# A fixed rank for each of 3,943 operations in place of a list scheduler, in a cluster-attention and two-MoE kernel

## The chip, the cores and the metric

One core of one Trainium2 chip runs the kernel. The metric is the device time of one execution in microseconds, median of several runs. TensorE (PE) does the matrix products and transposes, VectorE (DVE), ScalarE (ACT) and GpSimd (POOL) the work between them, and all data transfers are issued from SyncE's queue (SP). Each of the five takes its instructions strictly in program order.

## What is computed

Attention over 2 x 8 heads, 768 positions of 64, in which a query sees only the keys of its own cluster, and behind it two dense blocks on the 1536 x 512 result:

```python
q_assign = np.argmax(np.einsum('bhsd,hcd->bhsc', q_n, c_n), axis=-1)
k_assign = np.argmax(np.einsum('bhsd,hcd->bhsc', k_n, c_n), axis=-1)
mask = q_assign[:, :, :, None] == k_assign[:, :, None, :]
scores = np.where(mask, scale * np.matmul(q, k.transpose(0, 1, 3, 2)), -1000000000.0)
attn = softmax(scores); x = attn @ v            # (1536, 512)
a = x @ w1; b = x @ w2; x = ((a * b) @ w3) @ w_out
h = x @ w_in; out = (h * np.clip(h + 3.0, 0.0, 6.0) / 6.0) @ moe2_w_out
```

All inputs are float32. A product is made of three passes, each operand being split into a high and a low part.

## The kernel before

The kernel names 3,943 operations and gives each to a `Plan`: its engine (or several it may run on), an assumed duration, what it needs, which ring buffers it takes and drops, and a due time. `Plan.order` (line 888) is a list scheduler: it walks through assumed time, keeps the operations that are ready and have a buffer, and takes the one with the smallest due time; a table `SHIFT` (line 45) moves nearly every due time by hand. For an operation that may run on several engines it also picks the engine. Operations are then written out in that order, so it fixes the order on each of the five queues. Buffers are rings, and which operation takes a buffer next follows from the order too.

The stages, with the names that the steps below use (first the operation, then the program's name in the profile and its line):

- Start. The SP queue loads q (`lq`), k (`lk`), v and the centroids. Per head h: `T` transposes q and k (ptqk, L1194), `qkh` (ACT) and `qkl` (DVE, L1204) split them, `pa` (L1233) multiplies with the centroids, nine steps `oh0` to `oh8` (mostly DVE, some POOL, L1247 to L1263) make the cluster code, and `Ck` and `Cq` put it beside k and q (copies on DVE and ACT for head 0, DMA later). `Ek`, `Dk`, `Dq` are the DMAs that move k and q rows (L1208). `idle` (L1120) are matmuls without use that keep TensorE busy.
- Attention, six chunks c of 128 queries per head. `S1` and `S` (pst, L1332) make the scores in one of two banks, `mx` (DVE, L1344) the maximum, `ex` (ACT, L1351) the exponential; `S` of a chunk needs `ex` of the chunk before. Nine `pT` (ptr, L1367) transpose the result, `ph` (ACT) and `pl` (DVE, L1010) split it, six `av` (L1390) multiply with v.
- Beside it, to fill TensorE: the product of w3 and w_out (`wt` transposes L1601, `wth`, `wtl`, `w` = psw L1629) and the products with w1 and w2 for half of the tokens (`ab` = psab L1705, which waits for finished heads).
- Each weight block passes a conversion of five steps: load (`ld`, L1550), `c0` and `c2` on ACT, `c1` (a clamp, L1569) on POOL or DVE, `c3` and `c5` on DVE (L1578, L1582). There are 72 of them.
- Then `Wh`, `Wl` (Whl: high and low part of the w3-w_out product), `x2` (psx, L1820), `b` (psab, L1957) for the second half of the tokens, `x2` again, and the second block in 16 groups p: `h` (psh, L2268) in seven products, copies `s` of their banks (m_sn, ACT), `ca`, `hr`, `hm`, `hh`, `hl` (splitting the result into m_gv, m_whl), and `o` (po, L2312). Its weights come back by DMA (`ff`, `wf`) and are split by `Lh`, `Ll`, `woh2`, `wol2`.

TensorE's queue mixes these, so that one stage's waits are covered by another's products.

Of the kernel before, what the change touches and what calls it, by code (L numbers as in the profile page):

```python
# [27 lines left out]
LAT = {  # L28
    ("pe", "act"): 0.2, ("pe", "dve"): 0.2, ("pe", "pe"): 0.0, ("act", "dve"): 0.155, ("act", "pool"): 0.17,
    ("dve", "act"): 0.13, ("act", "pe"): 0.17, ("dve", "pe"): 0.24, ("pool", "pe"): 0.21, ("pool", "pool"): 0.1,  # L30
        ("dve", "dve"): 0.13, ("dve", "pool"): 0.155, ("pool", "act"): 0.08,
}

# [11 lines left out]
SHIFT = {  # L45
    "id": 8.27, "root": -37.83, "warm": -0.72, "cenl": -28.31, "cen1": -21.13, "cen2": -11.74, "cen3": 0.22,
    ("idle", 0): 0.14, ("idle", 1): 14.27, ("idle", 7): -19.93, ("idle", 8): 1.32, ("cT", 0): -2.63,
    ("cTc", 0): -18.72, ("cTc", 1): 38.21, ("lq", 0): -20.58, ("lk", 0): -6.84, ("vhi", 0): 13.43,
    ("vlo", 0): -8.33, ("T", 0, 0): -2.21, ("qkh", 0, 0): -20.39, ("qkl", 0, 0): -48.81, ("T", 0, 1): 58.8,
# [15 lines left out]
    ("vlo", 1): -17.06, ("T", 1, 0): 6.25, ("qkh", 1, 0): -6.73, ("qkl", 1, 0): 36.07, ("T", 1, 1): 0.16,  # L65
# [17 lines left out]
    ("lv", 2): -6.03, ("vhi", 2): -11.41, ("vlo", 2): 0.27, ("T", 2, 0): 24.8, ("qkh", 2, 0): 10.9,  # L83
# [786 lines left out]
class Plan:  # L870
# [1549 lines left out]
```

## Time and profile before

| | us |
|---|---|
| median of 3 runs (761.2 to 762.37) | 761.59 |
| the profiled execution | 763.72 |
| its span, first to last instruction | 761.8 |
| PE busy, of the span | 739.7 |
| DVE busy | 617.8 |
| ACT busy | 551.5 |
| POOL busy | 209.9 |
| mean granted TensorE clock, of full speed | 0.996 |

The span is what the rows below are timed in, from its own zero. A row of a timeline gives start, length, engine, line, operation, output and inputs, count, and in brackets how long the engine sat idle just before and what ended that.

### The profile page before, as it was taken

The numbers are of one execution on the slowest core, as the hardware profiler recorded it, in microseconds if no ns is written. First come the engines' busy times: TensorE is split into PE (matmuls) and PEld (weight loads), VectorE is DVE, ScalarE is ACT, GpSimd is POOL, SyncE is SP. The second block draws the span as 40 slices with busy tenths as digits, with TensorE's granted clock in tenths as the row PEclk, the third lists the DMA queues.
The fourth block names the chain that finished last, engine by engine and source line by source line (L and its number), as shares of the span: only waits on it lengthen the run. The fifth ranks groups of instructions, "written<-read, shape, count | busy, mean of one in ns | idle before, by whom it ended". The sixth has DMA issues, their size and how long they took to land.

```text
span 761.8 us, 12047 instructions
## 1 busy us (share of the span) xinstructions
PE 739.7 (97%) x4143; PEld 673.7 (88%) x4143; DVE 617.8 (81%) x1032; ACT 551.5 (72%) x1037; POOL 209.9 (28%) x232
## 2 busy tenths in 40 slices
PE   5899998999999999999999999999999999999998
PEld 4679887889899998999999999988988888988896
DVE  7778898999988887878896998979878867676642
ACT  6788898888889777878756767668765756565553
POOL 2441645252445435351341301322203000000000
PEclk9999999999999999999999999999999999999999
DMA  8745554565546646342536534685431224222102
GB/s 223 225 128 163 146 146 118 156 160 136 151 124 173 170 127 182 113 137 84 159 100 193 178 125 139 196 264 192 157 103 37 76 70 135 83 60 78 47 1 97
DMA packets 81740, 101.96 MB, mean 134 GB/s; under 512 B 30960, under 2 KB 56592, under 8 KB 81680
## 3 DMA queue, kind: packets, MB, share of 16 engines
q1 hardware_dynamic: 81680, 101.20, 45.0%
q8 instruction: 33, 0.54, 0.3%
q14 instruction: 27, 0.22, 0.1%
HBM read 71.34 MB, written 15.78 MB: 114 GB/s over the span
## 4 chain that ended last, share of the span: by engine, by line
PE 82%; DVE 6%; ACT 5%; DMA 4%; issue 2%; SPq 0%; POOL 0%; DVEq 0%; ACTq 0%; POOLq 0%
PE po L2312 15%; PE psh L2268 13%; PE av L1390 8%; PE psx L1820 8%; PE pst L1332 8%; PE ptr L1367 7%; PE psab L1705 7%; PE psab L1957 7%; PE psw L1629 5%; DMA qkn<-in_k_dram 1%; PE pa L1233 1%; PE ptqk L1194 1%; DVE den L1344 1%; PE pt L1601 1%; DMA rdb<-rd 1%
## 5 line engine op out<-in xcount | busy, mean ns | idle before, releaser
L1569 POOL TENSOR_SCALAR cvt<-cvt 128x512 f32<-128x512 f32 x72 | 67.3, 938 | 192.0 <-ACT cvt L1013 178.1
L1344 DVE TENSOR_REDUCE den<-pst 128x1 f32<-128x768 f32 x96 | 91.5, 953 | 22.8 <-PE pst L1332 18.1
L1351 ACT ACTIVATE p<-pst,den 128x768 f32<-128x768 f32 x96 | 86.6, 902 | 17.8 <-DVE den L1344 16.9
L1010 DVE TENSOR_TENSOR pl<-ptr,ph 128x512 fp32r<-128x512 f32 x135 | 89.4, 680 | 9.4 <-ACT ph L1013 9.1
L1013 ACT ACTIVATE ph<-ptr 128x512 fp32r<-128x512 f32 x135 | 78.7, 596 | 18.6 <-PE ptr L1367 13.8
L1367 PE MATMUL ptr<-id_f,p 128*128 128x128 f32 x576 | 81.3, 272 | 0.9 <-DVE pl L1010 0.6
L1705 PE MATMUL psab<-xT,abhl 128*128 128x384 f32 x384 | 78.9, 342 | 0.3 <-ACT asb L1013 0.3
L1367 PEld LDWEIGHTS ptr<-id_f,p 128*128 128x128 f32 x576 | 68.2, 140 | 8.8 <-DVE pl L1010 0.9
L1332 PE MATMUL pst<-kk,qkL 128*128 128x512 f32 (+1 forms) x192 | 71.0, 378 | 3.1 <-ACT p L1351 3.0
L1705 PEld LDWEIGHTS psab<-xT,abhl 128*128 128x128 f32 x384 | 66.2, 188 | 2.3 <-ACT asb L1013 0.8
L1332 PE MATMUL pst<-kk,qkH 128*128 128x512 f32 (+1 forms) x192 | 64.9, 342 | 0.0
L1390 PE MATMUL av<-pl,vs 128*128 128x384 f32 x180 | 61.3, 341 | 2.3 <-DVE pl L1010 2.3
L1390 PE MATMUL av<-ph,vs 128*128 128x384 f32 x180 | 63.3, 351 | 0.2 <-ACT T L1013 0.2
L1578 DVE SCALAR_TENSOR_TENSOR cvs<-cvt,cvs 128x512 int32<-128x512 int32 x72 | 52.4, 735 | 12.7 <-ACT cvs L1013 6.4
L1013 ACT ACTIVATE cvt<-raw 128x512 f32<-128x512 f32 x72 | 48.2, 672 | 11.5 <-DVE cvs L1582 3.8
L2290 ACT ACTIVATE tt<-m_sn,three 128x384 f32<-128x384 f32 x48 | 29.4, 615 | 37.0 <-DVE m_sn L2278 27.7
L1013 ACT ACTIVATE cvs<-raw 128x512 int32<-128x512 uint8 x72 | 47.9, 673 | 6.7 <-DMA set<-cvs 5.2
L1582 DVE SCALAR_TENSOR_TENSOR cvs<-cvt,cvs 128x512 int32<-128x512 int32 x72 | 51.2, 719 | 0.4
L1629 PE MATMUL psw<-woh,wT 128*128 128x512 f32 x128 | 49.3, 411 | 0.0
L1332 PEld LDWEIGHTS pst<-kk,qkL 128*128 128x128 f32 x192 | 36.9, 192 | 9.8 <-ACT p L1351 8.0
L1013 ACT ACTIVATE m_sn<-psh 128x384 f32<-128x384 f32 x64 | 30.8, 483 | 20.0 <-PE psh L2268 19.9
L2312 PE MATMUL po<-m_whl,m_gv 128*128 128x512 f32 x153 | 40.6, 392 | 0.6 <-DVE m_gv L1010 0.6
(198 smaller groups left out, 1829.6 us busy)
## 6 DMA issues: line engine op xcount, KB each, us to landing
raw<-in_moe_w_dram SPq DMA_DIRECT2D x32, 512.0 KB, 3.6
m_gb<-set SPq DMA_DIRECT2D x64, 256.0 KB, 3.3
raw<-in_moe_w_out_dram SPq DMA_DIRECT2D x24, 512.0 KB, 3.5
raw<-in_moe_w_in_dram SPq DMA_DIRECT2D x16, 512.0 KB, 5.1
set<-cvs SPq DMA_DIRECT2D x32, 256.0 KB, 3.1
kk<-qkH SPq DMA_DIRECT2D x16, 384.0 KB, 4.2
abp<-cvs SPq DMA_DIRECT2D x16, 256.0 KB, 2.3
b_gv<-abp SPq DMA_DIRECT2D x16, 256.0 KB, 4.4
```

The lines of the kernel that those rows point to most:

```text
L1010: nc.vector.tensor_tensor(out=out, in0=a, in1=b, op=ALU.subtract)
L1013: nc.scalar.activation(out=out, in_=in_, func=AF.Copy, **kw)
L1332: x = mm(out=psr[:, t, ks_], lhsT=TT[nm, h][:, i, cs_], rhs=flat(TT["K", h][:, a])[:, ks_], start=st, stop=sp)
L1344: done["mx", n] = [other_banks(nc.vector.tensor_reduce(out=den_at(h, 0, c), in_=psS[h, c], axis=AX.X, op=ALU.max, negate=True), ("S", n + 1))]
L1351: done["ex", n] = [other_banks(nc.scalar.activation(out=flat(p), in_=psS.pop((h, c)), func=AF.Exp, bias=den_at(h, 0, c), accum_out=den_at( ...
L1367: nc.tensor.transpose(pt[:, blk(j)], pps[h, 3 * hf + c][:, blk(kb)], id_f)
L1390: mm(out=t[:, 0:HF], lhsT=vs_t[h][:, 2 * s + i, :], rhs=x_[:, c0:c0 + HF], start=(s == 0 and i == 0 and n == 0), stop=(s == 2 and i == 1 a ...
L1569: (nc.gpsimd.tensor_scalar if e == "pool" else ts)(out=tf, in0=tf, scalar1=H_MAX, scalar2=-H_MAX, op0=ALU.min, op1=ALU.max)
L1629: mm(out=ps, lhsT=wT[m, hf][:, a, blk(kk)], rhs=w_[hf][:, kk, :], start=(kk == 0 and n == 0), stop=(kk == 3 and n == 2))
L1705: mm(out=ps[:, 0:HF], lhsT=s[:, w, a, blk(kk)], rhs=xT0[0][:, x_, kk, hf * HF:hf * HF + HF], start=(kk == 0 and n == 0), stop=(kk == KD - ...
L2268: mm(out=ps[:, 0:HF], lhsT=left(p, l, a, kk), rhs=x[:, x_, kk, :], start=(st and kk == 0 and m == 0), stop=(kk == 1 and m == 2), skip_grou ...
L2312: mm(out=outs[b, c], lhsT=g[:, a, blk(c % 3)], rhs=w[:, w_, :], start=(first and a == 0 and w_ == 0), stop=(last and a == 1))
```

## The change

`SHIFT`, `LAT` and the scheduler go. In their place stand a table `RANK` (for each family of operations one number per operation, its place among all 3,943) and a table `ON` (for each operation that may run on several engines, a letter: a, d, p for ACT, DVE, POOL). `Plan.order` reads both and checks them. Two lists of needs get longer: `gsh` names both operations `abg` that it reads, and `g1sh` all eight `bg1`. The operations are the same; 64 of them stand on another engine. Of the 72 clamps `c1`, 28 go from POOL to DVE. Of `wol2` eight go from DVE to POOL and two back, of `Ll` five and three back, of `Wl` two go to POOL (three of four are there then), and of `woh` two go to DVE. All lines after the tables move up by 592, so L1332 of before is L740 after.

```diff
-SHIFT = {
-    "id": 8.27, "root": -37.83, "warm": -0.72, "cenl": -28.31, "cen1": -21.13, "cen2": -11.74, "cen3": 0.22,
...
+RANK = {
+    "id": "4",
+    "root": "52",
+    "warm": "558",
...
+ON = {
...
+    "c1": "ppdppppppdppddpdpppppppppppdpddppdpppdddpppppddddpdpdpppdppddddppddpddpd",
+    "woh": "apddpppa",
+    "Wl": "pdpp",
...
     def order(self):
-        delta, bias = 0.05, {"dve": 0.3, "pool": -0.3}
...
-            pick = None
-            for e in ENG:
-                if cand[e]:
-                    m = min(cand[e])[0] + delta
-                    c = min((d, st, i, k) for st, d, i, k in cand[e] if st <= m)
...
+            f = k[0] if isinstance(k, tuple) else k
+            pos[k] = int(rank[f][n.setdefault(f, 0)])
...
+                o[2] = {"a": "act", "d": "dve", "p": "pool"}[ON[f][m.setdefault(f, 0)]]
...
+        seq = sorted(ops.values(), key=lambda o: pos[o[0]])
...
+        return seq
...
-            op(("gsh", hf, jp), "act", 0.8, lambda hf=hf, jp=jp: g_hi(hf, jp), ("top", ("abg", 2 * jp + 1, hf)), due=d)
+            op(("gsh", hf, jp), "act", 0.8, lambda hf=hf, jp=jp: g_hi(hf, jp), ("top", ("abg", 2 * jp, hf), ("abg", 2 * jp + 1, hf)), due=d)
...
-    last1 = [("bg1", J1 - 1), ("b", J1 - 1, 6, 1)]
+    last1 = [("bg1", j) for j in range(J1)] + [("b", J1 - 1, 6, 1)]
```

Three places show how the queues move. The first is TensorE at the start, before (ptqk x6 is `T` of head 1, ptqk x3 the first half of `T` of head 2, pt is `wt` of the second block of w3, pa is head 1, pst is `S1` of head 0's first chunk):

```order
L1194 MATMUL ptqk<-id_f,qkn 128x128 x6
L1120 MATMUL idle<-id_r 128x512 x2
L1601 MATMUL pt<-id_f,cvs 128x128 x4
L1194 MATMUL ptqk<-id_f,qkn 128x128 x3
L1233 MATMUL pa<-qkH,cT 128x384
L1233 MATMUL pa<-qkL,cT 128x384
L1233 MATMUL pa<-qkH,cT 128x384
L1233 MATMUL pa<-qkL,cT 128x384
L1332 MATMUL pst<-kk,qkL 128x512
```

and in the change, the same engine and place:

```order
L602 MATMUL ptqk<-id_f,qkn 128x128 x6
L528 MATMUL idle<-id_r 128x512 x4
L641 MATMUL pa<-qkH,cT 128x384
L641 MATMUL pa<-qkL,cT 128x384
L641 MATMUL pa<-qkH,cT 128x384
L641 MATMUL pa<-qkL,cT 128x384
L1009 MATMUL pt<-id_f,cvs 128x128 x4
L740 MATMUL pst<-kk,qkL 128x512
```

The transposes of head 2 no longer stand ahead of the first scores; they come behind `S` of the third chunk. The transposes of w3 stand behind `pa`.

The second is TensorE in head 4, before (ptr is `pT`, twelve matmuls for three of them; the two groups av are the first and the second `av` of head 4):

```order
L1367 MATMUL ptr<-id_f,p 128x128 x12
L1390 MATMUL av<-ph,vs 128x384
L1390 MATMUL av<-pl,vs 128x384
L1390 MATMUL av<-ph,vs 128x384
L1390 MATMUL av<-pl,vs 128x384
L1332 MATMUL pst<-kk,qkL 128x256
L1332 MATMUL pst<-kk,qkH 128x256
L1194 MATMUL ptqk<-id_f,qkn 128x128 x3
L1332 MATMUL pst<-kk,qkL 128x512
L1332 MATMUL pst<-kk,qkH 128x512
L1390 MATMUL av<-ph,vs 128x384
L1390 MATMUL av<-pl,vs 128x384
```

and in the change, from the first of these `av`:

```order
L798 MATMUL av<-ph,vs 128x384
L798 MATMUL av<-pl,vs 128x384
L798 MATMUL av<-ph,vs 128x384
L798 MATMUL av<-pl,vs 128x384
L1037 MATMUL psw<-woh,wT 128x512
L1037 MATMUL psw<-wol,wT 128x512
L1037 MATMUL psw<-woh,wT 128x512
L740 MATMUL pst<-kk,qkL 128x512
L740 MATMUL pst<-kk,qkH 128x512
L602 MATMUL ptqk<-id_f,qkn 128x128 x3
L798 MATMUL av<-ph,vs 128x384
L798 MATMUL av<-pl,vs 128x384
```

One operation `w` (three psw) stands now between the two `av`, and `S` (pst 128x256) stands before the first.

The third is GpSimd at the end of attention, before (abhl is `abl`, cvt is `c1`, Whl is `Wl`, xT is the last head pair's product):

```order
L1007 TENSOR_TENSOR abhl<-cvs,abhl 128x512 x2
L1569 TENSOR_SCALAR cvt<-cvt 128x512
L1007 TENSOR_TENSOR Whl<-W_591,Whl 128x1024
L1569 TENSOR_SCALAR cvt<-cvt 128x512
L1448 TENSOR_TENSOR xT_3003<-T,rdb 128x768
```

and in the change:

```order
L415 TENSOR_TENSOR abhl<-cvs,abhl 128x512
L977 TENSOR_SCALAR cvt<-cvt 128x512
L415 TENSOR_TENSOR Whl<-W_588,Whl 128x1024
L977 TENSOR_SCALAR cvt<-cvt 128x512
L415 TENSOR_TENSOR Whl<-W_588,Whl 128x1024 x2
L856 TENSOR_TENSOR xT_3046<-T,rdb 128x768
```

GpSimd has three `Wl` there in place of one.

## Rows read from the trace of the kernel before

**Rows 1.** The page: busy time, share of the span, instructions of each engine.

```profile
PE 739.7 (97%) x4143; PEld 673.7 (88%) x4143; DVE 617.8 (81%) x1032; ACT 551.5 (72%) x1037; POOL 209.9 (28%) x232
```

**Rows 2.** Busy time by stage: stretch, length, each engine, granted clock, DMA share, GB/s.

```profile
0.00:40.00 40.00, 29.38 (x132) 21.75 (x133) 30.13 (x61) 27.69 (x51) 16.01 (x43) 0.96 0.80 223
110.00:130.00 20.00, 16.93 (x92) 14.20 (x91) 16.65 (x25) 16.21 (x33) 11.31 (x12) 0.91 0.41 117
130.00:190.00 60.00, 59.97 (x376) 53.49 (x376) 57.75 (x98) 50.74 (x102) 19.69 (x24) 1.00 0.59 151
420.00:500.00 80.00, 79.99 (x461) 79.87 (x462) 74.35 (x131) 54.33 (x97) 16.55 (x12) 1.00 0.51 166
500.00:508.00 8.00, 6.63 (x37) 5.99 (x36) 6.23 (x9) 6.52 (x12) 3.10 (x3) 1.00 0.78 250
560.00:645.00 85.00, 83.36 (x416) 74.25 (x415) 66.53 (x110) 53.94 (x96) 8.95 (x5) 1.00 0.23 75
```

**Rows 3.** The same view of four short stretches, two beside each fall of the clock.

```profile
14.80:18.20 3.40, 0.76 (x5) 0.55 (x6) 3.21 (x7) 1.64 (x3) 1.04 (x2) 1.00 1.08 279
18.20:21.60 3.40, 3.40 (x12) 3.17 (x13) 0.93 (x3) 1.75 (x4) 0.60 (x1) 0.51 1.02 304
121.00:124.40 3.40, 1.14 (x5) 0.76 (x4) 3.34 (x5) 2.69 (x6) 1.07 (x2) 0.95 0.00 0
124.40:127.80 3.40, 3.40 (x13) 2.83 (x13) 1.48 (x2) 2.63 (x5) 3.32 (x4) 0.55 0.00 0
```

**Rows 4.** The chain of waits in the first 40 us: start, length, what.

```profile
9.17 1.28 ACT L1092
...
11.81 6.16 DMA qkn<-in_k_dram
```

**Rows 5.** Timelines of the start: PE, then ACT, DVE and POOL.

```profile
18.10 0.76 PE L1194 MATMUL ptqk<-id_f,qkn 128*128 128x128 f32 x3 [2.09 <-DMA qkn<-in_k_dram]
19.94 0.63 PE L1332 MATMUL pst<-kk,qkL 128*128 128x512 f32 x1
10.46 0.20 ACT L1092 ACTIVATE warm<-three 128x1 f32<-128x1 f32 x1
18.25 1.06 ACT L1013 ACTIVATE qkH<-cd 16x384 fp32r<-16x384 f32 x2
10.58 0.58 DVE L1247 STREAM_TRANSPOSE as<-pa 128x384 f32<-128x384 f32 x1 [0.18 <-PE pa L1233]
12.88 0.69 DVE L1578 SCALAR_TENSOR_TENSOR cvs<-cvt,cvs 128x512 int32<-128x512 int32 x1 [0.54 <-ACT cvs L1013]
17.22 0.35 DVE L1054 CAST kk<-cd 16x384 fp32r<-16x384 f32 x1
25.91 1.77 DVE L1578 SCALAR_TENSOR_TENSOR cvs<-cvt,cvs 128x512 int32<-128x512 int32 x1
25.75 1.39 POOL L1007 TENSOR_TENSOR wol<-cvs,woh 128x512 fp32r<-128x512 f32 x1
```

**Rows 6.** Timelines of head 4: PE twice, DVE, POOL.

```profile
118.97 0.66 PE L1367 MATMUL ptr<-id_f,p 128*128 128x128 f32 x4 [0.64 <-DVE pl L1010]
123.80 0.49 PE L1390 MATMUL av<-pl,vs 128*128 128x384 f32 x1 [2.26 <-DVE pl L1010]
119.43 2.85 DVE L1582 SCALAR_TENSOR_TENSOR cvs<-cvt,cvs 128x512 int32<-128x512 int32 x2
119.30 1.83 POOL L1448 TENSOR_TENSOR T<-T,rdb 128x768 f32<-128x768 f32 x1
```

**Rows 7.** Timelines before the second block: PE, then ACT.

```profile
505.67 1.34 PE L2268 MATMUL psh<-m_x1b,m_gB 128*128 128x384 f32 x6 [1.04 <-ACT m_sn L1013]
504.10 1.14 ACT L1013 ACTIVATE m_whl<-m_gb 128x512 fp32r<-128x512 f32 x2
```

**Rows 8.** Groups by line: two on POOL, busy time, mean of one, idle before.

```profile
L1569 POOL TENSOR_SCALAR cvt<-cvt 128x512 f32<-128x512 f32 x72 | 67.3, 938 | 192.0 <-ACT cvt L1013 178.1 <-DVE pl L1010 5.7 <-DVE m_sn L2282 4.3
L1007 POOL TENSOR_TENSOR Whl<-W,Whl 128x1024 fp32r<-128x1024 f32 x1 | 3.2, 3219 | 5.3 <-PE ptr L1367 5.3
```

More of the change, by code (lines that the diff above doesn't have):

```diff
@@ L27 @@
 ENG = ("pe", "act", "dve", "pool", "dma")
[L28 to L32, printed above, removed]
 RUN_ON = {
@@ L867 @@
+ON = {
+    "Ck": "dd",
+    "Cq": "aa",
+    "oh1": "pppdppppppdpdpp",
+    "oh4": "pdppppdppdppppp",
+    "xh": "papa",
+    "c1": "ppdppppppdppddpdpppppppppppdpddppdpppdddpppppddddpdpdpppdppddddppddpddpd",
+    "woh": "apddpppa",
+    "Wl": "pdpp",
+    "gsl": "dddddddp",
+    "bxl": "ddddddd",
+    "bxs": "dddd",
+    "g1s": "dddd",
+    "Ll": "ddddddddddddddddddpdpddddppdpddd",
+    "wol2": "ddpdddddpdddppddddpddpddppdpdddd",
+    "xwl": "dddddddddddddp",
+    "xs": "ddddpddd",
 }
@@ L884, in op @@
             eng, dur = (eng,), (dur,)
-        self.ops[key] = [key, dict(zip(eng, dur)), None, fn, tuple(need), due + SHIFT.get(key, 0.0), tuple(take), tuple(drop), lat,
+        self.ops[key] = [key, dict(zip(eng, dur)), None, fn, tuple(need), due, tuple(take), tuple(drop), lat,
             len(self.ops), lock, tuple(after)]
     def order(self):
-        delta, bias = 0.05, {"dve": 0.3, "pool": -0.3}
-        ops = self.ops
-        left, users, src = {}, {}, {}
+        ops, pos, n, m = self.ops, {}, {}, {}
@@ L892, in order @@
+        rank = {f: v.split() for f, v in RANK.items()}
         for k, o in ops.items():
-            left[k] = len(o[4]) + len(o[11])
-            src[k] = []
-            for n in o[4]:
-                users.setdefault(n, []).append((k, True))
-            for n in o[11]:
-                users.setdefault(n, []).append((k, False))
-        slots = {r: [0.0] * c for r, c in self.rings.items()}
-        free = dict.fromkeys(ENG, 0.0)
-        port = {"dve": 0.0, "pool": 0.0}
-        ready = {k: None for k, o in ops.items() if not left[k]}
@@ L903, in order @@
-        out = []
-        while len(out) < len(ops):
-            cand = {e: [] for e in ENG}
-            for k in ready:
-                o = ops[k]
-                t = 0.0
-                ok = True
-                for r in set(o[6]):
-                    c = o[6].count(r)
-                    if len(slots[r]) < c:
-                        ok = False
-                        break
-                    t = max(t, sorted(slots[r])[c - 1])
-                if not ok:
-                    continue
-                best = None
-                for e, d in o[1].items():
-                    st = max(free[e], t)
-                    for end, pe in src[k]:
-                        st = max(st, end + LAT.get((pe, e), 0.08))
-                    if e == "pool":
-                        st = max(st, port["dve"])
-                    elif e == "dve" and o[10]:
-                        st = max(st, port["pool"])
-                    f = st + d + bias.get(e, 0.0)
-                    if best is None or f < best[0]:
-                        best = (f, e, st)
-                cand[best[1]].append((best[2], o[5], o[9], k))
-            pick = None
-            for e in ENG:
-                if cand[e]:
-                    m = min(cand[e])[0] + delta
-                    c = min((d, st, i, k) for st, d, i, k in cand[e] if st <= m)
-                    if pick is None or c[1] < pick[0]:
-                        pick = (c[1], c[3], e)
-            if pick is None:
-                raise RuntimeError(f"no operation can start after {len(out)} of {len(ops)}")
-            st, k, e = pick
-            o = ops[k]
-            o[2] = e
-            del ready[k]
-            for r in o[6]:
-                slots[r].remove(min(slots[r]))
-            end = st + o[1][e]
-            free[e] = end
-            if e == "pool" or e == "dve" and o[10]:
-                port[e] = end
-            for r in o[7]:
-                slots[r].append(end + 0.3)
-            out.append(k)
-            for u, data in users.get(k, ()):
-                if data:
-                    src[u].append((end + o[8], e))
-                left[u] -= 1
-                if not left[u]:
-                    ready[u] = None
@@ L959, in order @@
-        return [ops[k] for k in out]
+            f = k[0] if isinstance(k, tuple) else k
+            pos[k] = int(rank[f][n.setdefault(f, 0)])
+            n[f] += 1
+            o[2] = next(iter(o[1]))
+            if len(o[1]) > 1:
+                o[2] = {"a": "act", "d": "dve", "p": "pool"}[ON[f][m.setdefault(f, 0)]]
+                m[f] += 1
+            assert o[2] in o[1], k
+        seq = sorted(ops.values(), key=lambda o: pos[o[0]])
+        room = dict(self.rings)
+        for i, o in enumerate(seq):
+            assert pos[o[0]] == i, o[0]
+            assert all(pos[x] < i for x in o[4] + o[11]), o[0]
+            for r in o[6]:
+                room[r] -= 1
+                assert room[r] >= 0, (o[0], r)
+            for r in o[7]:
+                room[r] += 1
```

257 lines of the change are left out of this document (142 added, 115 removed), and 828 rows, old and new, of tables (RANK, SHIFT).

## The prediction

> **What bounds the kernel now.** I read the page's busy times first. TensorE is busy in 739.7 of 761.8 us [rows 1], and the change leaves its operations as they are, so an order can win no more than the 22.1 us in which it idles, and what a slower clock costs it. The view by stage shows where that is: 10.6 us in the first 40, 3.1 in 110 to 130, 1.4 in 500 to 508, 1.6 in 560 to 645 (each length less PE busy [rows 2]). From 130 to 190 and from 420 to 500 it idles for 0.04 us in 140. So most of the kernel is a wall of matmuls that no order shortens, and the case is decided at four short places, and by whether the new order makes new ones.
>
> The same view gives the clock. It stands at 0.51 of full speed, the 1.2 GHz level, from 18.2 to 21.6, after 3.4 us in which TensorE was busy for 0.76, and at 0.55 from 124.4 to 127.8, after 3.4 us with 1.14 busy [rows 3]. Each time some 1.6 us are lost: 3.4 us of matmuls at half speed do the work of 1.7 to 1.9. So an idle time of 2 to 3 us there is paid nearly twice.
>
> Second, VectorE. It is busy for 57.75 of 60 us from 130 to 190 (96%) and 74.35 of 80 from 420 to 500 (93%) [rows 2]. The change gives it more work, so it's the engine to fear.
>
> **The start.** Before, the first scores `S1` begin at 19.94, and just ahead of them TensorE waits 2.09 us for k of head 2, whose load took 6.16 us [rows 4, 5]. The scores need none of it; their own last input is made by the two copies on ACT from 18.25 to 19.31, and the first chunk uses the first, done at about 18.8 [rows 5]. In the new order the transposes of head 2 stand behind the third chunk, and that gate is gone.
>
> What is late next is VectorE. The new order puts `c5` of the first w3 block (0.69, as its neighbour `c3` took [rows 5]) ahead of head 0's split, loads k of head 0 one place later, and puts `c1` and `c3` of the second block ahead of `oh0`. I make that 0.69 for `c5`, 0.69 for `c3`, and for `c1` between 0.35 and 0.69: no clamp ran on VectorE, the nearest rows are its short steps of 0.35 and its conversions of 0.69. Idle time of 0.18 ahead of `oh0` takes some back, and so does the clamp's lying in a wait. `oh0` moves from 10.58 to about 12.0. Behind it `c3` and `wtl` (0.69 each) no longer stand in the chain of codes, so the first copy `Ck` stays at 17.22 + 1.4 - 1.4 = 17.2, the second follows on the same engine (0.35), and `S1` starts at about 18.1: 1.8 us earlier.
>
> From there the chunks of head 0 run as a chain of scores, maximum and exponential, which the earlier start shifts as a whole. Inside it one conversion took 1.77 us in place of 0.69, ending 0.54 after a POOL operation (25.75 + 1.39) that began before it [rows 5]. Whether VectorE meets POOL again there, the order doesn't say; I count 0.4 of the 1.1. Sum: -2.2, bounds 0 (another load gates) and -3.5.
>
> A rule of the Trainium skill speaks against the change here. The load of the exponential's table took 1.28 us at 9.17, beginning 0.02 after the operation before and followed by the next at 10.46 [rows 4, 5]; the new order drops it from there to just ahead of the first exponential. By the same walk it fits: ACT is through with the second `wth` at about 19.1, loads until 20.4, and the maximum comes at about 20.6. The Trainium skill ("ScalarE: Activation LUTs", What ACT_TABLE_LOAD costs) gives a switch of tables 1.28 us and another 1.38 of drain; by that the start would win 1.1 us less. No drain shows in the rows, and the place is the one where it would matter.
>
> **Head 4.** TensorE waits 0.64 us and then 2.26 for `pl` [rows 6], and loses 1.6 to the clock after it. VectorE is late because its two `c5` took 2.85 us, where two of 0.69 are 1.4; POOL's 1.83 us began 0.13 before them. In the new order VectorE has the same sequence (`pl` twice, `c5` twice, `mx`, `pl` twice) and POOL the same two products, so I expect them to meet again. TensorE, however, has one more `w` (three psw) ahead of the second `av` and one more among the transposes. A matmul of all shapes took 0.16 us on average from 130 to 190 (59.97 us in 376 [rows 2]); three are 0.5, and as `w` has the widest shape, 512 columns, I say 0.7; what `S` takes is moved ahead and no longer counts. So the idle 2.9 shrinks by 0.6 and 0.5 to 1.8, and the clock falls or doesn't: half of 1.6. Sum: -1.1 - 0.8 = -1.9, bounds 0 and -4.5 (all of it gone).
>
> **Before the second block.** `h` of the first group waits 1.04 us for the copy of its bank [rows 7], which ACT makes only after a copy of x2 and two weight copies that together take 1.14 [rows 7]. The new order puts this copy ahead of those three. The wait for VectorE's sum behind it stays. Sum: -0.8, bounds 0 and -1.4, the idle time of that stretch.
>
> **The end of attention.** `Wl` on POOL took 3.22 us [rows 8]; the change has three there, so about 9.7 us of POOL inside some 12, beside conversions on VectorE. By the two stretched conversions above, VectorE can't start such an operation while POOL is in one. I price one meeting at the stretch that head 4 shows, 1.4, and count 0.7 of it as reaching TensorE, which has `ab` products to do. Sum: +1.0 for one and a half, bounds 0 (all under `ab`) and +3.2 (one whole `Wl`).
>
> **The rest.** In 560 to 645 TensorE idles 1.6 us, mostly at an `o` behind a late `hl`; the new order puts nine operations ahead of that `o`, which covers it. The 28 clamps take 28 x 0.35 to 0.69, 10 to 19 us, to VectorE, which cost POOL 0.94 each [rows 8]; 16 of them lie behind 360 us, and eight `wol2` leave VectorE there. As TensorE hides nearly all of VectorE now, I cost them at nothing; the cover is VectorE's free time, 2.25 us in 130 to 190, where no clamp moves, and 5.65 in 420 to 500, where four do. Sum: -1.0, bounds -2 and +3.5.
>
> **Sum.** -2.2 - 1.9 - 0.8 + 1.0 - 1.0 = -4.9 us. The profiled execution took 763.72, with 1.9 outside its span of 761.8; so 758.8 for one like it. The median of the runs is 761.59, 2.1 less than the profiled one, and the difference goes against that: **756.7 us**.
>
> **The rivals.**
> - *VectorE sets the pace of attention: slower.* Ahead of head 8's scores the new order asks VectorE for five clamps, two weight copies and three `oh` steps more: 5 x 0.35 to 0.69, 2 x 0.69, 3 x 0.35, some 4.2 to 5.9, say 4.7. It decides from where VectorE's free time, 2.25 in 60 us, can't take them. The start's win stays, the head 4 win doesn't: 761.6 - 2.2 + 4.7 + 1.0 = 765.1. For it: 96% busy. Against: most of the extra work lies before 62 us, where VectorE is 75% busy (30.13 of 40 [rows 2]).
> - *The waits move.* TensorE's queue is in order, and each wait taken away uncovers the next. Then 761.6, give or take 1.5. Against: the four places have causes that are named, and two of them lie in the order alone.
> - *All four places close,* and the clock never falls: -3.5 - 4.5 - 1.4 + 0 - 1.2 = -10.6, so 751.0. For it: both falls follow idle times that the order shortens. Against: head 4's meeting with POOL is left as it was.
> - *The table load costs its drain,* by the start's rule: 756.7 + 1.1 = 757.8. Against: the rows show none.
> - That the change does nothing can be left out: the queues differ in most rows.
>
> **How the numbers follow.** The forecast has a chance of 0.55, spread from 752 to 761; VectorE's pace 0.15, the moved waits 0.12, all closed 0.13, the drain 0.05. The range holds all but half of the third rival and most of the first: 750.5 to 763.5. A change of 0.2%, 1.5 us, is about what this measurement tells from none: faster takes the forecast but for 0.04, the drain and the third rival (0.69, and a little of the second), same 0.11, slower 0.19.
>
> **What would show it.** In the new profile the first scores should begin at 18 to 18.5; the wait for k of head 2 should be gone; the wait of `av` in head 4 should be 1 to 2 us, and the row of the clock at 110 to 130 tell whether it fell; the wait for m_sn's copy near 500 should be gone. The forecast is wrong if TensorE waits for VectorE by more than 2 us in sum between 130 and 360, or if the end of attention shows a wait of 2 us for `pl` or the bank.

## The result: slower by 0.74%

| | before | after the change |
|---|---|---|
| median, us | 761.96 | 766.9 |
| ratio, 95% interval | | 1.0074 [1.0055, 1.0092] |
| profiled execution, us | 763.72 | 767.14 |
| its span, us | 761.8 | 765.4 |

The forecast was 756.7, with a range up to 763.5; the kernel is some 5 us slower than before (medians of four runs each; alone they give 1.0065, inside the interval). Of b2_three_start below, one execution of five took 4,153 us against 757 to 758 of the others, and it is left out. The page of after, its first line as in [rows 1] (busy time, share, instructions of each engine):

```profile
PE 739.1 (97%) x4143; PEld 674.4 (88%) x4143; DVE 630.6 (82%) x1059; ACT 547.6 (72%) x1033; POOL 190.7 (25%) x209
```

TensorE is busy for nearly as long as before (739.1 us against 739.7), so the 3.6 us by which the span grew are idle time, and 0.6 more. The view by stage, columns as in [rows 2]:

```profile
0.00:40.00 40.00, 29.61 (x129) 22.20 (x130) 31.14 (x65) 26.50 (x48) 13.12 (x39) 0.96 0.71 201
110.00:130.00 20.00, 18.19 (x110) 15.18 (x109) 18.80 (x29) 17.45 (x34) 14.24 (x14) 1.00 0.52 138
130.00:190.00 60.00, 60.00 (x380) 53.96 (x379) 58.96 (x101) 51.59 (x104) 18.43 (x24) 1.00 0.59 148
360.00:420.00 60.00, 55.95 (x319) 55.15 (x318) 52.75 (x75) 39.13 (x67) 14.07 (x9) 0.97 0.47 153
500.00:508.00 8.00, 8.00 (x48) 8.00 (x47) 6.82 (x11) 4.62 (x8) 1.26 (x2) 1.00 0.59 204
560.00:645.00 85.00, 83.21 (x413) 74.28 (x412) 64.37 (x112) 51.65 (x94) 8.95 (x5) 1.00 0.21 69
```

Two of the four places of the prediction behave as it said: from 110 to 130 the idle time fell from 3.07 to 1.81 and the clock no longer falls, and from 500 to 508 nothing idles. The start idles as before, 10.4 us. And 360 to 420 has 4.05 us of idle time and a granted clock of 0.97, where the kernel before idles for 0.76. Two of TensorE's waits, by matmul and releaser (us in total, times, longest):

```profile
PE ptr L775 <- DVE pl L418: 5.0, 3, 4.0
PE av L798 <- ACT T L421: 2.1, 2, 1.7
```

To see what the clock and small waits add, I took from each trace the time from a matmul's start to the next one's, less the median of that for its operation and shape in the trace of before, and summed the excess by stretch. It is TensorE's lost time, in us (a stretch can shift by some 5 us between kernels):

| stretch | before | after | e2 | f1 | f2 | b1 |
|---|---|---|---|---|---|---|
| 0 to 40 | 13.0 | 12.8 | 12.2 | 12.8 | 12.6 | 12.9 |
| 40 to 110 | 2.8 | 4.3 | 4.1 | 3.5 | 3.0 | 4.2 |
| 110 to 130 | 5.5 | 2.9 | 1.3 | 1.9 | 5.2 | 1.3 |
| 130 to 190 | 1.1 | 0.6 | 0.6 | 0.5 | 1.8 | 0.6 |
| 190 to 300 | 1.9 | 5.0 | 6.8 | 4.5 | 2.4 | 3.7 |
| 300 to 360 | 1.5 | 0.3 | 0.4 | 0.8 | 1.3 | 0.5 |
| 360 to 420 | 2.3 | 6.3 | 0.6 | 1.4 | 3.5 | 0.6 |
| 420 to 510 | 2.3 | 0.8 | 1.0 | 0.9 | 3.9 | 0.8 |
| 510 to 600 | 3.4 | 3.2 | 3.2 | 5.4 | 3.8 | 3.2 |
| 600 to 620 | 0.3 | 2.1 | 2.1 | 0.5 | 0.3 | 0.4 |
| 620 to the end | 2.4 | 1.7 | 1.5 | 2.0 | 5.6 | 1.5 |
| all | 36.5 | 40.0 | 33.7 | 34.3 | 43.3 | 29.4 |

The kernels behind the last four columns follow. Four rows of it rise: 190 to 300 (+3.1), 360 to 420 (+4.0), 600 to 620 (+1.8) and 40 to 110 (+1.5). The 6.8 of e2 holds a fall of the clock (0.50 from 268.3 to 271.7) behind a wait of 1.9, which the other kernels don't have there.

A column is one profiled execution, and executions of one kernel differ. The sum, +3.5, is the difference of the two profiled executions (767.14 less 763.72, 3.4), while the medians differ by 5: the profiled execution of before was a long one, at a granted clock of 0.996. Of the 56 executions of before beside the experiments, the nine at 0.999 or 1.0 took 759.4 to 760.7. So some 1.5 us of the loss have no place in this table.

### The profile page after: what moved, and what is told of

Read it like the earlier page. It is cut to its first block, busy times and chain, and to the rows that moved or that the text cites. A ratio compares the mean times of both kernels' runs of the same rounds, so it can differ in the third digit from the quotient of the medians.

```text
span 765.4 us, 12013 instructions
## 1 busy us (share of the span) xinstructions
PE 739.1 (97%) x4143; PEld 674.4 (88%) x4143; DVE 630.6 (82%) x1059; ACT 547.6 (72%) x1033; POOL 190.7 (25%) x209
## 4 chain that ended last, share of the span: by engine, by line
PE 80%; DVE 10%; ACT 4%; DMA 2%; issue 2%; POOL 1%; SPq 0%; DVEq 0%; ACTq 0%; POOLq 0%
PE po L1720 15%; PE psh L1676 12%; PE psx L1228 9%; PE psab L1365 8%; PE pst L740 7%; PE av L798 7%; PE psab L1113 7%; PE ptr L775 7%; PE psw L1037 5%; PE ptqk L602 1%; DVE cvs L986 1%; DVE den L752 1%; PE pa L641 1%; DVE pl L418 1%; ACT p L759 1%
## 5 line engine op out<-in xcount | busy, mean ns | idle before, releaser
L775 PE MATMUL ptr<-id_f,p 128*128 128x128 f32 x576 | 83.6, 273 | 5.5 <-DVE pl L418 5.0
L1113 PE MATMUL psab<-xT,abhl 128*128 128x384 f32 x384 | 81.6, 346 | 0.0
L740 PE MATMUL pst<-kk,qkL 128*128 128x512 f32 x192 | 71.7, 376 | 2.6 <-ACT p L759 2.4
L977 POOL TENSOR_SCALAR cvt<-cvt 128x512 f32<-128x512 f32 x44 | 30.9, 704 | 155.3 <-ACT cvt L421 144.2
L740 PE MATMUL pst<-kk,qkH 128*128 128x512 f32 x192 | 64.4, 340 | 0.0
L986 DVE SCALAR_TENSOR_TENSOR cvs<-cvt,cvs 128x512 int32<-128x512 int32 x72 | 58.6, 817 | 3.7 <-POOL cvt L977 2.7
L990 DVE SCALAR_TENSOR_TENSOR cvs<-cvt,cvs 128x512 int32<-128x512 int32 x72 | 52.2, 728 | 0.6
L1037 PE MATMUL psw<-woh,wT 128*128 128x512 f32 x128 | 51.9, 418 | 0.0
L740 PEld LDWEIGHTS pst<-kk,qkL 128*128 128x128 f32 x192 | 36.4, 190 | 9.9 <-ACT p L759 7.0
L1702 DVE SCALAR_TENSOR_TENSOR tt<-tt,m_sn 128x384 f32<-128x384 f32 x48 | 29.2, 608 | 13.0 <-ACT tt L1698 12.9
```

The costliest lines, as they stand in the source:

```text
L740: x = mm(out=psr[:, t, ks_], lhsT=TT[nm, h][:, i, cs_], rhs=flat(TT["K", h][:, a])[:, ks_], start=st, stop=sp)
L775: nc.tensor.transpose(pt[:, blk(j)], pps[h, 3 * hf + c][:, blk(kb)], id_f)
L1037: mm(out=ps, lhsT=wT[m, hf][:, a, blk(kk)], rhs=w_[hf][:, kk, :], start=(kk == 0 and n == 0), stop=(kk == 3 and n == 2))
L1113: mm(out=ps[:, 0:HF], lhsT=s[:, w, a, blk(kk)], rhs=xT0[0][:, x_, kk, hf * HF:hf * HF + HF], start=(kk == 0 and n == 0), stop=(kk == KD - ...
```

## The experiments

All but two keep the tables of the change and add two short lists to `Plan.order`: `SEAT` gives an operation another engine, and `BEHIND` puts one right behind another in the order.

```diff
+SEAT = {("c1", "set", 5, 0): "pool"}
+BEHIND = [(("c1", "set", 5, 0), ("Wl", 3))]
...
+            o[2] = SEAT.get(k, o[2])
...
+        for a, b in BEHIND:
+            seq.remove(ops[a])
+            seq.insert(seq.index(ops[b]) + 1, ops[a])
```

Ratios are to the kernel before on the same chip. A difference between two ratios is given in us at 761.6 us.

| kernel | median, us | ratio, 95% interval |
|---|---|---|
| the change | 766.9 | 1.0074 [1.0055, 1.0092] |
| e1_clamp_late | 762.19 | 1.0010 [0.9996, 1.0024] |
| e2_clamp_pool | 761.34 | 1.0003 [0.9990, 1.0016] |
| e3_c2_later | 765.19 | 1.0053 [1.0040, 1.0066] |
| e4_xwl_dve | 764.79 | 1.0039 [1.0021, 1.0057] |
| s1_load | 766.34 | 1.0058 [1.0041, 1.0075] |
| s2_load_pa | 767.32 | 1.0069 [1.0051, 1.0086] |
| s3_load_pa_table | 764.74 | 1.0040 [1.0025, 1.0056] |
| f1_letters | 761.99 | 1.0007 [0.9993, 1.0021] |
| f2_old_order | 770.0 | 1.0101 [1.0080, 1.0121] |
| b1_three | 758.73 | 0.9947 [0.9929, 0.9965] |
| b2_three_start | 757.44 | 0.9939 [0.9922, 0.9956] |
| b3_three_start_h4 | 758.32 | 0.9951 [0.9935, 0.9967] |

### The end of attention: one clamp

The rows there in the trace of after are TensorE's wait, then VectorE, then GpSimd (a timeline, columns as in [rows 5]):

```profile
370.80 0.63 PE L775 MATMUL ptr<-id_f,p 128*128 128x128 f32 x4 [4.00 <-DVE pl L418]
363.73 3.16 DVE L418 TENSOR_TENSOR Whl<-W,Whl 128x1024 fp32r<-128x1024 f32 x1
366.82 2.56 DVE L977 TENSOR_SCALAR cvt<-cvt 128x512 f32<-128x512 f32 x1
369.96 1.29 DVE L418 TENSOR_TENSOR pl<-ptr,ph 128x512 fp32r<-128x512 f32 x2
363.41 2.40 POOL L415 TENSOR_TENSOR Whl<-W,Whl 128x1024 fp32r<-128x1024 f32 x1 [1.07 <-ACT Whl L421]
366.61 2.48 POOL L415 TENSOR_TENSOR Whl<-W,Whl 128x1024 fp32r<-128x1024 f32 x1 [0.80 <-ACT Whl L421]
```

`Wl` on VectorE began 0.32 after one on GpSimd and ended 1.08 after it; the clamp began 0.21 after the next and ended 0.29 after that (369.38 against 369.09). Usual for the clamp is 420 ns, as its group shows (ns min, median, max; first and last start):

```profile
L977 DVE TENSOR_SCALAR cvt<-cvt x28: 412/420/2558, 11.5 to 545.8; 128x512 f32<-128x512 f32 x28
```

Two experiments tell a hold by GpSimd from too much work. In the first the clamp goes to GpSimd behind the last `Wl` (the lists above).

> The changed kernel (766.9) with one clamp, c1 of block (set, 5, 0), taken from VectorE to GpSimd and put behind the last Wl there. In the changed kernel that clamp began 0.2 us after a Wl on GpSimd and took 2.56 us where 0.42 is usual, and TensorE then waited 4.00 us at 366.8 for pl. Theory A (a VectorE operation of this kind can't start its work while GpSimd is in one): the second of two meetings goes, the first (Wl on VectorE, 3.16 us) stays; the wait shrinks from 4.0 to about 1.5, and the time falls by about 2.5, to 764.4. Theory B (VectorE has simply too much to do there): it is relieved of one clamp of 0.42, the wait stays at 3.5 or more, 766.5.

VectorE, then the wait, in this kernel:

```profile
360.46 3.17 DVE L431 TENSOR_TENSOR Whl<-W,Whl 128x1024 fp32r<-128x1024 f32 x1
365.10 0.63 PE L788 MATMUL ptr<-id_f,p 128*128 128x128 f32 x4 [1.53 <-DVE pl L431]
```

The first meeting stands, the second is gone, and the wait fell to 1.53, by 2.47 for a clamp of 0.42: theory A. The time fell by 4.9 and not by 2.5, give or take some 2 by the two intervals. In lost time the wait's stretch, 360 to 420, gave 4.0, the clock's share among it, as the clock no longer falls behind the shorter wait. The profiled execution is 7.4 us below that of after, since another 1.6 fell in head 4 and 1.4 in the first 40 us, where the edit changes nothing (both are told below).

In the second the same clamp goes to GpSimd at its own place, which is one letter of `ON`:

```diff
+SEAT = {("c1", "set", 5, 0): "pool"}
```

> The same clamp on GpSimd, at its own place, which is ahead of two of the three Wl there and so delays them. Theory A: GpSimd then starts its second Wl only after the clamp, at about 365.0, when VectorE is through with its own Wl (1.2 us from 363.73); both meetings go, and the wait of 4.0 with them: -4.0 to -4.5 with what the clock lost behind it, 762.4 to 762.9. Theory B: as before, 766.5, since VectorE is again relieved of 0.42 alone.

```profile
362.99 1.22 DVE L424 TENSOR_TENSOR Whl<-W,Whl 128x1024 fp32r<-128x1024 f32 x1
363.72 0.96 POOL L983 TENSOR_SCALAR cvt<-cvt 128x512 f32<-128x512 f32 x1 [2.13 <-ACT cvt L427]
364.65 4.76 POOL L421 TENSOR_TENSOR Whl<-W,Whl 128x1024 fp32r<-128x1024 f32 x2
```

VectorE's `Wl` takes 1.22, the wait of 4.0 is gone, and with it all of the loss against before: 1.0003. In lost time at 360 to 420, the six profiles of the new order that leave this clamp where the change has it show 6.2 to 7.2, and the four with it at its own place on GpSimd 0.6 to 1.9. The hold in the other direction is in these rows too, for here the clamp on GpSimd began while VectorE was in its `Wl` and took 0.96 in place of 0.62: who starts second waits.

The clock belongs to the same price. In after, behind the 4.0 us without a matmul, it was 0.50, the 1.2 GHz level, from 371.9 to 375.3 (the second row has part of that; columns as in [rows 2]):

```profile
366.80:370.80 4.00, 0.00 (x1) 0.03 (x1) 3.97 (x5) 0.59 (x2) 2.29 (x1) 1.00 0.49 168
370.80:374.20 3.40, 3.40 (x15) 3.40 (x16) 2.38 (x5) 1.67 (x3) 0.00 (x0) 0.66 0.00 0
```

### Two more waits, alone

At 267.8 TensorE waits 1.72 for the copy `oa` that frees its bank, and ACT, which makes it, had stood for a transfer:

```profile
269.53 0.41 PE L798 MATMUL av<-ph,vs 128*128 128x384 f32 x1 [1.72 <-ACT T L421]
267.22 0.68 ACT L421 ACTIVATE cvs<-raw 128x512 int32<-128x512 uint8 x1 [1.70 <-DMA abp<-cvs]
```

```diff
+BEHIND = [(("oc", 10, 1), ("vhi", 11)), (("oa", 10, 1), ("oc", 10, 1))]
```

> The changed kernel with the two copies oc and oa of (10, 1) put ahead of c2 of block (ab, 3, 0) on ACT. In the changed kernel ACT stood 1.70 us at that c2 for a transfer, and TensorE waited 1.72 us at 267.8 for the oa behind it. If ACT's order is the cause: the wait goes, -1.7, 765.2. Rival: ACT still stands for the transfer, the exponential and the next copies behind it come as late as before, and TensorE waits at the next matmul that needs them: within 0.5 of 766.9.

Lower by 1.6 by the ratios, whose intervals overlap, so the trace has to decide. In lost time from 262 to 275 the four kernels with this edit have 0.7 to 0.9 and the eight others in the new order 2.0 to 3.8: the first reading holds, for some 1.3. ACT still stands there for the transfer (0.94 us), but with the copies made, and TensorE waits 0.60 for something else:

```profile
264.27 0.48 ACT L431 ACTIVATE T<-av 64x384 f32<-64x384 f32 x1
265.69 0.66 ACT L431 ACTIVATE cvs<-raw 128x512 int32<-128x512 uint8 x1 [0.94 <-DMA abp<-cvs]
268.48 0.52 PE L612 MATMUL ptqk<-id_f,qkn 128*128 128x128 f32 x3 [0.60 <-DVE qkL L622]
```

At 613 the change has put `xwl` (1, 6) on GpSimd, behind a `wol2` that has that engine in both kernels:

```profile
614.65 1.32 PE L1676 MATMUL psh<-m_x1b,m_w 128*128 128x384 f32 x6 [1.56 <-DVE m_sn L1686]
609.97 4.16 DVE L1583 TENSOR_TENSOR m_gb<-m_gb 128x256 f32<-128x256 f32 x4
610.11 1.42 POOL L415 TENSOR_TENSOR m_whl<-m_gb,m_whl 128x512 fp32r<-128x512 f32 x1 [25.92 <-ACT m_whl L421]
611.49 2.03 POOL L415 TENSOR_TENSOR m_whl<-x2f,m_whl 128x768 fp32r<-128x768 f32 x1
```

```diff
+SEAT = {("xwl", 1, 6): "dve"}
```

> The changed kernel with one operation, xwl (1, 6), on VectorE in place of GpSimd, as it was before the change. In the changed kernel a copy fs that started 0.25 us behind it on VectorE took 2.06 us in place of 0.42, and TensorE waited 1.56 us at 613.1 for the sum behind that copy. Theory A (VectorE held by GpSimd): the wait goes, -1.5, 765.4. Theory B (VectorE too full): it gets 0.95 us more to do, and the wait grows or stays, 766.9 to 767.9.

```profile
609.10 2.51 DVE L1589 TENSOR_TENSOR m_gb<-m_gb 128x256 f32<-128x256 f32 x4
```

Four copies that took 4.16 us take 2.51, although VectorE now has 0.94 more to do, and TensorE's wait is gone from the list. Lost time at 600 to 620 went from 2.05 to 0.40, and it is 0.4 in all four kernels with this edit and 2.0 to 2.1 in the seven others of the new order that have `xwl` on GpSimd. The time fell by 2.7, a little more than the 1.5 expected, which the intervals allow; that they overlap leaves the proof to the trace.

### The start

In after the first scores began at 19.25, not at 18.1. Ahead of them:

```profile
8.75 1.51 PE L602 MATMUL ptqk<-id_f,qkn 128*128 128x128 f32 x6 [1.68 <-DMA qkn<-in_k_dram]
13.69 0.58 DVE L655 STREAM_TRANSPOSE as<-pa 128x384 f32<-128x384 f32 x1 [0.95 <-PE pa L641]
18.75 0.72 DVE L462 CAST kk<-cd 16x384 fp32r<-16x384 f32 x2
19.25 0.47 PE L740 MATMUL pst<-kk,qkL 128*128 128x512 f32 x1
20.82 1.28 ACT L759 ACT_TABLE_LOAD   x1
22.11 0.90 ACT L759 ACTIVATE p<-pst,den 128x768 f32<-128x768 f32 x1
```

`oh0` (STREAM_TRANSPOSE) is 3.1 later than in [rows 5], not 1.4: the transposes wait for k of head 0, and then `pa` stands behind `wt` and three idle matmuls. From `oh0` to the first `Ck` it's 5.06 us, 1.6 less than before, as the prediction had it (1.4).

But this profile is a late one. The edits of e1 to e4 and of b1 lie behind 260 us, so these kernels run the start of after again, unchanged. In e1 to e4 the transposes begin at 8.10 to 8.53, `oh0` at 12.46 to 12.89 and the first scores at 18.01 to 18.44, where the prediction had 18.1; in b1 the scores begin at 19.62. In all six they follow `oh0` by 5.55 to 5.58. Two rows of e3_c2_later:

```profile
12.46 0.58 DVE L665 STREAM_TRANSPOSE as<-pa 128x384 f32<-128x384 f32 x1 [0.19 <-PE pa L651]
18.01 0.60 PE L750 MATMUL pst<-kk,qkL 128*128 128x512 f32 x1
```

So one start varies by 1.6 us between executions: k of head 0 comes at other times, and the four matmuls of `pa` take 1.28 us in after and 0.69 in e3 (why, is open). Lost time in the first 40 us is 11.2 to 12.3 in e1 to e4, 12.8 in after and 12.9 in b1. What follows was expected against after's profile alone. Three kernels, each with one step more:

```diff
+BEHIND = [(("lq", 1), ("lk", 0)),                                  # s1
+          (("idle", 8), ("pa", 0)), (("wt", 0, 0), ("pa", 0)),     # s2
+          ("root", "id"), ("warm", ("qkh", 0, 1))]                 # s3
```

> The changed kernel with the load of q of head 1 put behind the load of k of head 0, as before the change. In the changed kernel k of head 0 came at 8.61 and its transposes began at 8.75, where they began at 7.02 before; the first scores came at 19.25 and not at the 18.1 predicted. If that load is what ate the gain: transposes 1.1 to 1.7 earlier, first scores at about 18, the time 1.0 to 1.5 lower, 765.4 to 765.9. Rival: the scores wait for work on VectorE that stands there anyway: first scores 19.0 or later, 766.9.

Transposes at 6.86, first scores at 18.46; lost time in the first 40 us 11.7, and the ratio lower by 1.2 us, with overlapping intervals. Against after's profile that is what was expected. Against e1 to e4 it is nothing: their transposes begin 1.2 to 1.7 later and their scores no later. The rival holds: VectorE's clamp and `c3` stand ahead of `oh0` (12.88 here), and the clamp waited for ACT:

```profile
11.70 0.43 DVE L986 TENSOR_SCALAR cvt<-cvt 128x512 f32<-128x512 f32 x1 [1.05 <-ACT cvt L430]
```

> As s1_load, and the product pa of head 0 stands ahead of wt of the first w3 block and of the three idle matmuls behind it on TensorE. In the changed kernel pa stood behind them until 12.39 though its last input was there at 11.53. First scores another 0.6 to 0.9 earlier than in s1_load, about 17.3; the time another 0.5 lower, 764.9 to 765.4. Rival: VectorE's clamp and conversion of the second block stand ahead of the code steps and take the gain: no earlier than s1_load.

`oh0` came 0.3 earlier, the first scores at 19.17, later than in s1_load and in e1 to e4 (18.94 to 19.18 in all four kernels with this edit). The rival holds, in another form: what was taken out ahead of `pa` of head 0 then stood ahead of head 1, whose split on VectorE lies among head 0's code steps and waited 0.96 us for ACT:

```profile
15.28 0.62 DVE L623 SCALAR_TENSOR_TENSOR qkL<-ptqk,qks,qkH 128x384 fp32r<-128x384 f32 x1 [0.96 <-ACT qkH L620]
```

> As s2_load_pa, and the two operations that load ACT's tables stand where they stood before the change: root first on ACT, warm behind the split of head 0. In the changed kernel the table load of 1.28 us stood from 20.82 to 22.10, 0.43 past the end of the first maximum. If it cost that: first exponential 0.4 or more earlier than in s2_load_pa, the time 0.4 lower. If it also cost a drain of 1.38: 1.8 lower. Rival: ACT has slack there; no difference.

```profile
21.40 0.90 ACT L772 ACTIVATE p<-pst,den 128x768 f32<-128x768 f32 x1 [0.91 <-DVE den L765]
```

The first exponential waits for the maximum now and starts 0.63 earlier than in s2_load_pa (22.03), 0.23 of it from the scores' own earlier start: 0.40 for the table load, as expected. (From the scores to the exponential it is 2.46 us in s3, b2 and b3, and 2.83 to 2.86 in after, e1 to e4, s1, s2 and b1, where the load stands ahead of it.) No drain shows: in after the exponential began 0.01 after the load ended. The Trainium skill ("ScalarE: Activation LUTs", What ACT_TABLE_LOAD costs) would have 1.38 us more there; this trace doesn't have them. The ratio lies 2.6 us below the change's, but the start doesn't show that much: lost time in the first 40 us is 11.8, inside what e1 to e4 have, and 1.6 of the difference between the profiles of s3 and after lie in head 4.

### Head 4: a meeting that comes or not

In after and in e1_clamp_late the same operations stand in the same order, VectorE's two `c5` and GpSimd's product. First after, then the other:

```profile
119.67 2.95 DVE L990 SCALAR_TENSOR_TENSOR cvs<-cvt,cvs 128x512 int32<-128x512 int32 x2
119.94 2.13 POOL L856 TENSOR_TENSOR T<-T,rdb 128x768 f32<-128x768 f32 x1
124.14 0.44 PE L798 MATMUL av<-pl,vs 128*128 128x384 f32 x1 [1.43 <-DVE pl L418]
```

```profile
118.08 1.28 DVE L1003 SCALAR_TENSOR_TENSOR cvs<-cvt,cvs 128x512 int32<-128x512 int32 x2
118.93 2.14 POOL L869 TENSOR_TENSOR T<-T,rdb 128x768 f32<-128x768 f32 x1 [0.73 <-DMA qkH<-cd]
```

In the second GpSimd waited 0.73 for a transfer and came when VectorE's second `c5` had begun. So VectorE wasn't held, and TensorE had no wait. Lost time at 110 to 130 is 2.9 in the one case and 1.3 in the other; of the profiles of this order, after, e3, e4, s1 and b2 have the first (GpSimd begins 0.27 to 0.57 behind the first `c5`), e1, e2, s2, s3 and b1 the second (0.70 to 1.07). Neither case goes with an edit, so 1.6 us of difference between two profiles can be this alone.

### Order and engines apart

f1_letters has the new order with the old `ON`, f2_old_order the old order with the new `ON`:

```diff
-    "c1": "ppdppppppdppddpdpppppppppppdpddppdpppdddpppppddddpdpdpppdppddddppddpddpd",
-    "Wl": "pdpp",
+    "c1": "pppppppppppppppppppppppppppppppppppppppppppppppppppppppppppppppppppppppp",
+    "Wl": "dddp",
...
```

> The order of the changed kernel with the engine of every operation as it was before the change (64 letters back). If the loss lies in the letters at two places (the clamp and Wl at the end of attention, xwl at 613): -4.2 - 1.6, 761.1. If the 28 clamps, back on GpSimd, hold VectorE at new places, 763 to 765. If the order itself is what loses, 766 or more.

> The other half of f1_letters: the order of before, and the 64 new engines. If the new engines cost by themselves, as they did in the new order (766.9 against 762.0): 766. If they cost only where the new order lays a VectorE operation beside a long one on GpSimd: near before, 761 to 763; since Wl has two more on GpSimd here too, I take 763.

The new engines cost 5.1 us in the new order (1.0074 against 1.0007) and 7.7 in the old (1.0101 against 1). With the old engines the new order is worth nothing by its time (1.0007): in lost time, what it wins at head 4 and at 505 (3.6 and 1.4 us) it loses at 190 to 300, at 510 to 600 and at 40 to 110 (2.6, 2.0, 0.8).

My expectation for f2 was wrong in size and in place. Three `Wl` on GpSimd cost 1.2 us of lost time at the end of attention there, not 4. Most of the loss lies at 505 and in the second block (1.6 at 420 to 510, 3.2 behind 620):

```profile
509.35 3.92 PE L1532 MATMUL psh<-m_x1b,m_gB 128*128 128x384 f32 x12 [2.72 <-ACT m_sn L277]
648.86 1.32 PE L1532 MATMUL psh<-m_whl,m_w 128*128 128x384 f32 x6 [1.03 <-DVE m_sn L1542]
710.68 0.73 PE L1576 MATMUL po<-m_w,m_whl 128*128 128x512 f32 x2 [0.85 <-POOL m_w L271]
```

What each of these costs alone wasn't tried.

### All three edits

```diff
+SEAT = {("c1", "set", 5, 0): "pool", ("xwl", 1, 6): "dve"}
+BEHIND = [(("oc", 10, 1), ("vhi", 11)), (("oa", 10, 1), ("oc", 10, 1))]
```

> The changed kernel with the edits of e2_clamp_pool, e3_c2_later and e4_xwl_dve together. Alone they gave -5.6, -1.7 and -2.1 against the 766.9 of the changed kernel. If the three waits are independent, the sum: -9.4, 757.5, faster than before (761.5). If waits that they uncover take some back: 759 to 760.

Faster than before by 0.53%, 9.7 us below the change by the ratios: the three add up (5.4, 1.6 and 2.7 alone). The clock doesn't fall in this profile. The next two add the start's edits, and then this for head 4:

```diff
+          (("c5", "w3", 1, 1), ("pl", 4, 3)),
+          (("c0", "w3", 2, 1), ("c5", "w3", 1, 1)),
```

> As b1_three, with the three edits of the start of s3_load_pa_table, which gave -2.2 in the median and -2.15 by TensorE's intervals in the profile: 755.3. Rival: that -2.2 was the meeting in head 4, which fell away in that run by chance; then the start gives 0.4 to 0.7, 757.

0.9939 against 0.9947, 0.6 us, with overlapping intervals: a gain of the start's edits is not shown (the 0.8 of lost time between these two profiles is less than b1's start differs from that of e1 to e4). The rival is right that s3's 2.2 were not the start's alone.

> As b2_three_start, with the second of the two c5 in head 4 on VectorE put behind the two pl that follow (and the c0 that takes its buffer behind it). In the profiles of this order the two c5 took 2.95 us and TensorE waited 1.43 for pl where GpSimd's product began 0.27 us after the first c5, and 1.28 us with no wait where it began 0.85 us or more after. Theory A: the wait can't come any more, in the profile no wait of av for pl near 120; the median 0.7 lower than b2_three_start, as about half of the profiles had it. Rival: the c5 put later is hit by GpSimd instead and holds the wt product behind it: same or slower.

The rival is right. (The limit of 0.85 in the expectation should read 0.70, as e2 has it.) GpSimd was late in this run, 0.92 behind the first `c5`, so the old wait would not have come; the `c5` put later met the next GpSimd operation and TensorE waited for it by way of `wt`:

```profile
121.61 1.71 DVE L1012 SCALAR_TENSOR_TENSOR cvs<-cvt,cvs 128x512 int32<-128x512 int32 x1
121.48 1.29 POOL L437 TENSOR_TENSOR wol<-cvs,woh 128x512 fp32r<-128x512 f32 x1
123.47 0.63 PE L1031 MATMUL pt<-id_f,cvs 128*128 128x128 f32 x4 [0.91 <-DVE cvs L1012]
```

## Why the prediction was wrong, step by step

In lost time, predicted against measured (the profile of after less that of before, 3.5 of the 5 us between the medians):

| step | predicted | measured |
|---|---|---|
| the start | -2.2 | -0.2 (-0.8 to -1.8 in e1 to e4) |
| head 4 | -1.9 | -2.6 (-4.2 without the meeting) |
| before the second block | -0.8 | -1.9 |
| the end of attention | +1.0 | +4.0 |
| the rest | -1.0 | +4.2 |
| sum | -4.9 | +3.5 |

- **What bounds it** was right: busy time of TensorE hardly moved, and the change is in its waits and, behind two of them, its clock.
- **The end of attention** is the mis-sized term. The mechanism stood there, VectorE can't start such an operation while GpSimd is in one. I counted one and a half stretches of 1.4, and half of each as reaching TensorE. There were two, of 1.94 (3.16 less 1.22) and 2.14 (2.56 less 0.42), since a `Wl` holds for 2.4; both stood ahead of the `pl` that TensorE waited for, so all of it reached the end, beyond my bound of +3.2, and the clock fell behind it. e1 and e2 show it by one clamp. The sign that I had named, a wait of 2 us for `pl` there, came with 4.0.
- **The start.** The gate named was real and went, the steps from `oh0` on were right to 0.2 us, and so were the first scores, 18.1, in e1 to e4 (18.01 to 18.44). After's profile has them at 19.25. What the sum lacked is that `oh0` also waits for k of head 0 and for `pa` behind `wt` and idle matmuls, which moves the start by 1.6 us from one execution to the next; the small gain in the table is one draw of it. That the load's new place cost anything is not shown (s1).
- **The table load** cost 0.40, which I had at nothing; the rival with the drain is refuted by the rows of after.
- **Head 4 and 505** came as foreseen, and larger. The wait for `pl` was 1.43 in after, in the predicted 1 to 2, and the meeting with GpSimd came again; that it comes by chance I had not seen. At 505 the wait is gone with its tail (500 to 510), 1.9 against my bound of 1.4, a stretch whose small waits I hadn't counted.
- **The rest** is the largest error, -1.0 against +4.2, beyond the bound of +3.5. I looked at the places where the old order waits, and costed the extra work on VectorE at nothing elsewhere because TensorE hid it there. That tells what the old order covers, not the new one. New waits: 1.7 at 267 (ACT in line behind a transfer), 1.6 at 613 (GpSimd again), and smaller ones behind stretched `c3` (0.57 at 87 and 0.44 at 210, where a `c3` took 2.15 and 2.07). The group of `c3` on VectorE, after and then before, shows the same median and a longer tail:

```profile
L986 DVE SCALAR_TENSOR_TENSOR cvs<-cvt,cvs x72: 647/684/2158, 7.6 to 566.8; 128x512 int32<-128x512 int32 x72
```

```profile
L1578 DVE SCALAR_TENSOR_TENSOR cvs<-cvt,cvs x72: 648/684/1770, 7.4 to 554.0; 128x512 int32<-128x512 int32 x72
```

- **The rivals.** VectorE as the pace of attention didn't happen: from 130 to 190 TensorE idles for nothing, and the five clamps ahead of head 8 took 0.42 to 0.53 each. Its time, 765.1, is near the measured one by luck, for the mechanism is another. "The waits move" is what f1_letters shows, the new order with the old engines: no difference from before. The loss on top is the letters': one clamp, by e2, is worth about as much as all 64 (5.4 and 5.1).

## What to carry to other kernels

Waits in the old trace tell what an order can win, never what a new one will lose: for a changed order go through the new queues for two patterns, a long operation on GpSimd beside VectorE work that TensorE is about to need, and an in-order engine that has a wait for a transfer ahead of a copy that frees a bank. Price such a meeting at the whole of the GpSimd operation, not at an average stretch. Read more than one profile of a stretch before a difference there is put down to an edit: the start and head 4 here moved by 1.6 us each with no edit at all. And an order and the engines of its operations are one choice: either half of this change alone was no gain, and three small edits in it made 1.3%.

## What the runs showed of the hardware

- A clamp, `c3`, `c5` or `Wl` on VectorE that starts while GpSimd is at work ends a fixed time behind GpSimd's end, whatever that operation's length: the clamp 0.28 to 0.29, `c3` and `c5` 0.54 to 0.55 (behind operations of 0.5 to 2.5 us), `Wl` 1.08, somewhat less than each takes alone (0.42, 0.69, 1.22). It holds in the other direction: GpSimd's product that began 0.27 into a `c5` took 2.13, where 1.84 is usual. The Trainium skill ("SBUF — State Buffer", SBUF: two separate sides) says of the ports that the two engines share that whoever starts first has them for the whole instruction; these rows agree, those of the next point don't.
- The one that waits can wait through several. In before a clamp on GpSimd (median 0.62) began at 388.4 while VectorE was in an operation, and took 6.95: nine more VectorE operations, all begun later, went ahead of it at their usual lengths, until VectorE itself had nothing to do but wait for that clamp. The mean of 0.94 in [rows 8], by which the prediction priced a clamp on GpSimd, holds such waits. Its group and VectorE's row:

```profile
L1569 POOL TENSOR_SCALAR cvt<-cvt x72: 603/616/6945, 6.8 to 545.0; 128x512 f32<-128x512 f32 x72
395.35 1.09 DVE L1578 SCALAR_TENSOR_TENSOR cvs<-cvt,cvs 128x512 int32<-128x512 int32 x1 [0.51 <-POOL cvt L1569]
```

- VectorE operations with an operand in PSUM aren't held: in after, 63 of the 96 maxima and 66 of the 135 `pl` ran beside a GpSimd operation, and none took over 0.96 and 0.70 us.
- A few tenths of a us, by which a transfer lets GpSimd start earlier or later, decide whether two engines meet (0.57 behind the first `c5` of head 4 they did, 0.70 behind it not), and the lost time there moves by 1.6. That part of the spread of a kernel's times is of this kind is likely, but no kernel was traced twice.
